# Attention and a gated MLP on one core: scores in bursts of three units, a lent pair of banks

## The chip, the core and the metric

The kernel runs on one core of a Trainium2 chip. A core has a matmul engine (TensorE, shown as PE, with its weight loads as PEld), a vector engine (VectorE, DVE), an activation engine (ScalarE, ACT), a general engine (GpSimd, POOL), and a queue that issues most transfers (SyncE, SP). Each engine takes its own instructions in the order in which they are written; between engines, semaphores say when a result is there or a buffer free. Matmuls write their results into PSUM, which here is used as eight banks of 128 partitions x 512 float32; only ACT and DVE read them from there in this kernel. The metric is the device time of one execution in microseconds (us); lower is better.

## The reference

Grouped attention (16 query heads, 4 key heads, 384 tokens, head size 64, batch 8), whose output is the input of an MLP with a spatial gate:

```python
scores = scale * np.matmul(q, k.transpose(0, 1, 3, 2))
attn = np.exp(scores - scores.max(-1, keepdims=True))
attn = attn / (attn.sum(-1, keepdims=True) + 1e-09)
x = np.matmul(attn, v)               # heads side by side: B x S x 1024
h = np.maximum(x @ w_in, 0.0)        # 1024 -> 1024
u, v = h[..., :512], h[..., 512:]
v_n = (v - mean(v)) / np.sqrt(var(v) + 1e-06)
v_s = np.einsum('ts,bsd->btd', w_spatial, v_n) + b_spatial[None, :, None]
out = (u * v_s) @ w_out              # 512 -> 1024
```

## The kernel before

Everything is float16 on the matmul engine. The order of the work is written out by hand: one loop over steps `n`, each of which issues, on PE, a piece of the attention and then a number of columns of matmuls of the MLP of an earlier batch, out of a generator (`stream`, `run_fill`).

**Attention.** A batch has six sets `m` (token tile `qt`, half of the heads `j`), and a set has three units `t`, one for each tile of 128 keys, so 18 units a batch (`NU`) and 144 in all. `scores(n)` (L224) makes one unit: two matmuls of 64 rows x 512 columns, one in each half of the array, into a tile of two banks, and one exp of 1024 columns on ACT. `weigh(b, m, hh)` (L242) is done twice for each set: twelve matmuls of 65 columns into the one bank of `ps_av`, then on DVE a reciprocal `r` and a multiplication that writes `x16`. Its weights are the exps, all three units of a set.

In the first batch one unit is issued a step; from step 18 on, two units at every even step (L599 to L601).

**The gated MLP.** For each batch: three `v_tile`s (L288; eight matmuls of 512 columns, relu on DVE, then mean and variance on DVE), four `u_block`s (L358; eight matmuls of 384 columns, relu on ACT; the first batch has three `u_tile`s instead, L337), in the middle of the first of them `normal` (L311: Ln and Exp of three columns on ACT, `nmr` on DVE, three normalisations on POOL), four `gate`s (L375; three matmuls of 384 columns, an addition on DVE, a multiplication on POOL), and six `project`s (L395; four matmuls of 512 columns, a copy on DVE for the first half of a row and on ACT for the second, and the transfer out). The first v-tile of the next batch stands between the gates and the projections (L447). "A group" is below the matmuls that fill one bank before it is read out.

**PSUM.** Eight banks: two tiles of two banks for the scores (`ps_sc`, L59), one for the weighing (L60), and three single banks, in turn, for all else (`ps_ck`, L61): the transposes of q, k, x and of the spatial weights, the warm-up matmuls and the groups of the MLP. A pool hands its buffers out in a ring, so a tile waits for the last reader of the tile that had its buffer before.

**Around it.** `keep_warm` (L502) issues four matmuls into a bank that nobody reads, at steps 0 to 9, 14 and 15. Loads, casts and transposing transfers are issued at fixed steps (`at`, L489) on POOL's and SP's queues; the PE transposes of the first batches at fixed steps too (`turn_at`, L494).

Of the kernel before, what the change touches and what calls it, by code (L numbers as in the profile page):

```python
# [12 lines left out]
ALU = mybir.AluOpType  # L13
# [4 lines left out]
def kernel(  # L18
# [37 lines left out]
    moe = ctx.enter_context(tc.tile_pool(name="moe", bufs=2))  # L56
    small = ctx.enter_context(tc.tile_pool(name="small", bufs=4))
    ops = ctx.enter_context(tc.tile_pool(name="ops", bufs=4))
    ps_sc = ctx.enter_context(tc.tile_pool(name="ps_sc", bufs=2, space=PSUM))  # L59
    ps_av = ctx.enter_context(tc.tile_pool(name="ps_av", bufs=1, space=PSUM))  # L60
    ps_ck = ctx.enter_context(tc.tile_pool(name="ps_ck", bufs=3, space=PSUM))  # L61


    stage = {}
# [118 lines left out]
        return qTs[b, j]  # L183

    def k_transposes(b, j, eng):
        ps = ps_ck.tile([P, S], FP16, name=f"kps_{b}_{j}", tag="ck")
        for t in range(NT):
            nc.tensor.transpose(
                ps[:, t * P : (t + 1) * P],
                k16s[b][:, j, t].rearrange("p h d -> p (h d)"),  # L190
                ident16,
            )
        eng(k_tile(b)[:, j], ps)

    def q_transposes(b, j, t, *engs):
        w = G // len(engs)
        for x, eng in enumerate(engs):
            ps = ps_ck.tile([P, w * P], FP16, name=f"qps_{b}_{j}_{t}_{x}", tag="ck")
            for i in range(w):
                nc.tensor.transpose(  # L200
                    ps[:, i * P : (i + 1) * P],
                    q16s[b, j][:, t, x * w + i].rearrange("p h d -> p (h d)"),
                    ident16,
                )
            eng(q_tile(b, j)[:, t, x * w * P : (x + 1) * w * P], ps)
# [13 lines left out]
        )  # L219


    aTs, avs, x16s, xts = {}, {}, {}, {}

    def scores(n):  # L224
        b, r = divmod(n, NU)
        m, t = divmod(r, NT)
        qt, j = divmod(m, 2)
        if t == 0:
            aTs[b, m] = att.tile([P, NT, 2, 512], FP16, name=f"aT_{b}_{m}", tag="aT", bufs=3)
        sc = ps_sc.tile([P, 2, 512], FP32, name=f"sc_{b}_{m}_{t}", tag="sc")  # L230
        for hh in range(2):
            half = slice(hh * D, (hh + 1) * D)
            nc.tensor.matmul(  # L233
                sc[:, hh],
                kTs[b][half, j, t * P : (t + 1) * P],
                qTs[b, j][half, qt],
                start=True,
                stop=True,
            )
        nc.scalar.activation(aTs[b, m][:, t], sc, AF.Exp, scale=scale)  # L240

    def weigh(b, m, hh):  # L242
        qt, j = divmod(m, 2)
        av = ps_av.tile([P, G, D + 1], FP32, name=f"av_{b}_{m}_{hh}", tag="av")
        for i in range(G):
            for t in range(NT):
                nc.tensor.matmul(  # L247
                    av[:, i, :],
                    aTs[b, m][:, t, hh, i * P : (i + 1) * P],
                    v1[b % 2][:, 2 * j + hh, t, 0 : D + 1],  # L250
                    start=(t == 0),
                    stop=(t == NT - 1),
                )
        if m == 0 and hh == 0:
            x16s[b] = att.tile([P, NT, NB, P], FP16, name=f"x16_{b}", tag="x16")
        r = small.tile([P, G, 1], FP32, name=f"r_{b}_{m}_{hh}", tag="r")
        nc.vector.reciprocal(r, av[:, :, D : D + 1])  # L257
        blk = 4 * j + 2 * hh
        nc.vector.tensor_tensor(  # L259
            x16s[b][:, qt, blk : blk + 2].rearrange("p k (i d) -> p (k i) d", i=2),  # L260
            av[:, :, 0:D],
            r.to_broadcast([P, G, D]),
            ALU.mult,
        )
# [5 lines left out]

    def x_transposes(b, m):
        qt, j = divmod(m, 2)
        ps = ps_ck.tile([P, 4, P], FP16, name=f"xps_{b}_{m}", tag="ck")
        for i in range(4):
            nc.tensor.transpose(ps[:, i], x16s[b][:, qt, 4 * j + i], ident16)  # L275
        nc.vector.tensor_copy(x_tile(b)[:, qt, 4 * j : 4 * j + 4], ps)
# [11 lines left out]
    def v_tile(b, st):  # L288
        if st == 0:
            mvs[b] = small.tile([P, NT, 2], FP32, name=f"mv_{b}", tag="mv")  # L290
            v_rs[b] = []
        pv = ps_ck.tile([P, 512], FP32, name=f"pv_{b}_{st}", tag="ck")
        for kt in range(NB):
            nc.tensor.matmul(  # L294
                pv,
                x_tile(b)[:, st, kt],
                w_in16[:, kt, DH:DFF],
                start=(kt == 0),
                stop=(kt == NB - 1),
            )  # L300
            if kt < NB - 1:
                yield 512
        vr = moe.tile([P, DH], FP32, name=f"vr_{b}_{st}", tag="vr", bufs=4)
        nc.vector.tensor_scalar(vr, pv, 0.0, None, op0=ALU.max)  # L304
        stats = small.tile([P, 6], FP32, name=f"stats_{b}_{st}", tag="stats")
        nc.vector.bn_stats(stats, vr)  # L306
        nc.vector.bn_aggr(mvs[b][:, st, :], stats)
        v_rs[b].append(vr)
        yield 512
# [26 lines left out]

    def u_tile(b, st):  # L337

        pu = ps_ck.tile([P, NM, P], FP32, name=f"pu_{b}_{st}", tag="ck")
        for m in range(NM):  # L340
            for kt in range(NB):
                if st == 1 and m == 1 and kt == 0:
# [7 lines left out]
                )  # L350
                if m < NM - 1 or kt < NB - 1:
                    yield P
        nc.vector.tensor_scalar(
            uT_tile(b)[:, :, st * P : (st + 1) * P], pu, 0.0, None, op0=ALU.max
        )
        yield P

    def u_block(b, m):  # L358
        pu = ps_ck.tile([P, 512], FP32, name=f"pu_{b}_{m}", tag="ck")
        for kt in range(NB):  # L360
            nc.tensor.matmul(  # L361
                pu[:, 0:S].rearrange("p (t s) -> p t s", t=NT),
                w_in16[:, kt, m * P : (m + 1) * P],
                x_tile(b)[:, :, kt],
                start=(kt == 0),
                stop=(kt == NB - 1),
            )
            if m == 0 and kt == 3:
                normal(b)
            if kt < NB - 1:  # L370
                yield S
        nc.scalar.activation(uT_tile(b)[:, m, :], pu[:, 0:S], AF.Relu)
        yield S

    def gate(b, m):  # L375
        if m == 0:
            gTs[b] = moe.tile([P, NM, S], FP16, name=f"gT_{b}", tag="gT")
        psp = ps_ck.tile([P, 512], FP32, name=f"psp_{b}_{m}", tag="ck")
        for st in range(NT):
            nc.tensor.matmul(  # L380
                psp[:, 0:S],
# [5 lines left out]
            if st < NT - 1:  # L387
                yield S
        g = moe.tile([P, S], FP32, name=f"g_{b}_{m}", tag="g", bufs=4)
        nc.vector.tensor_tensor(g, psp[:, 0:S], bias_b, ALU.add)  # L390
        by = nc.vector if b == B - 1 and m % 2 else nc.gpsimd
        by.tensor_tensor(gTs[b][:, m, :], g, uTs[b][:, m, :], ALU.mult)  # L392
        yield S
# [1 line left out]
    def project(b, tt, half):  # L395
# [5 lines left out]

        cuts = (512, 768, 1024) if last and tt == NT - 1 and half else (512 * half, 512 * half + 512)
        for i, (lo, hi) in enumerate(zip(cuts, cuts[1:])):
            po = ps_ck.tile([P, 512], FP32, name=f"po_{b}_{tt}_{half}_{i}", tag="ck")
            for m in range(NM):
                nc.tensor.matmul(  # L406
                    po[:, 0 : hi - lo],
# [4 lines left out]
                )  # L412
                if m < NM - 1:
                    yield hi - lo
            (nc.scalar.copy if half and not i else nc.vector.tensor_copy)(  # L415
                osb[:, lo:hi], po[:, 0 : hi - lo]
            )
            if last:
                nc.sync.dma_start(rows[:, tt, lo:hi], osb[:, lo:hi])
# [58 lines left out]
        w_stage["ws16"] = t16  # L478

    def ws_transposes(st):  # L480
        ps = ps_ck.tile([P, S], FP16, name=f"wps_{st}", tag="ck")
# [15 lines left out]

    by_dve, by_act = nc.vector.tensor_copy, nc.scalar.copy

    warm = ps_ck.tile([P, 512], FP32, name="warm", tag="ck")  # L500

    def keep_warm(n):  # L502
        for _ in range(n):
            nc.tensor.matmul(warm[:, 0:P], ident16, ident16, start=True, stop=True)  # L504

# [27 lines left out]
    for j in range(2):  # L533
        for t in (1, 2):
            turn_at(3 * (2 * t + j) - 3, q_transposes, 0, j, t, by_dve)
    for n in (*range(10), 14, 15):
        turn_at(n, keep_warm, 4)
    at(9, cast_k, 1, pool)
    at(10, cast_q, 1, 0, pool)
# [48 lines left out]
    def run_fill(cols):  # L588
        nonlocal owed
        owed += cols  # L590
        while owed > 0:
            owed -= next(fill, 1e9)

    for n in range(total + 6):
        for f, args in todo.pop(n, []):
            f(*args)
        if n + 1 < NU:
            scores(n + 1)
        elif n >= NU and n % 2 == 0 and n < total:  # L599
            scores(n)  # L600
            scores(n + 1)  # L601
        for hh in range(2):
            b, r = divmod(n - 3 - hh, NU)
            if n >= 3 + hh and r % 3 == 0 and b < B:
                weigh(b, r // 3, hh)
        for f, args in turns.pop(n, []):
            f(*args)
        if n < NU + 3:

            run_fill(HV / 4 if 10 <= n < 14 else 2 * HV / 5 if 16 <= n else 0)  # L610
        elif n < 2 * NU + 4:
            run_fill((4 * HV + NM * NT * S + 6 * NM * 512) / (NU + 4 - 3))
        else:
            run_fill(COLS / NU)
    for _ in fill:
        pass
    assert not todo and not turns
# [1 line left out]
_INS = ['q', 'k', 'v', 'moe_w_in', 'moe_w_spatial', 'moe_b_spatial', 'moe_w_out']  # L619
# [26 lines left out]
```

## Time and profile before

| | |
|---|---|
| runs, median (lowest to highest) | 253.76 us (253.17 to 254.05), 3 runs |
| the profiled execution | 253.12 us |
| its span, first to last instruction | 251.3 us |
| instructions in it | 6020 |
| granted TensorE clock, mean over the span | 1.00 |
| exps (L240) | 144, 139.6 us busy on ACT |
| scores (L233) | 288 matmuls, 45.0 us busy on PE |

The profile is one execution. Its span is 1.8 us shorter than its time, which has what lies around the program. A row of a group gives busy time, the mean duration of one in ns, and then the idle time of the engine just before it and who ended it. Matmuls are pipelined: one takes 379 ns from start to end at 512 columns while the next one starts much earlier, so the mean duration is not the step. The chain of waits follows the work that ended last backwards and gives time to each instruction from its start to the next one's.

### The profile page before, as it was taken

How to read it: one execution, taken by the hardware profiler on the slowest of the kernel's cores; microseconds unless marked ns; L12 is line 12 of the kernel's file. 1: busy time of each engine (PE TensorE's matmuls, PEld its weight loads, DVE VectorE, ACT ScalarE, POOL GpSimd, SP SyncE). 2: the span in 40 equal slices, each digit the busy share in tenths (PEclk: the TensorE clock that was granted, in tenths of full speed). 3: DMA queues.
4: the chain of work that ended last, by engine and by line, in shares of the span. 5: the costliest groups of instructions: out<-in, count | busy, mean ns of one | idle time of the engine just before them, and what ended most of it. 6: DMA issues, size and time to landing. Idle time of an engine off the chain costs nothing.

```text
span 251.3 us, 6020 instructions
## 1 busy us (share of the span) xinstructions
PE 240.9 (96%) x2430; PEld 125.7 (50%) x2430; DVE 139.7 (56%) x368; ACT 168.2 (67%) x215; POOL 98.3 (39%) x142
## 2 busy tenths in 40 slices
PE   7898998999999999999999999999999999999883
PEld 7564657534455444544455445544455445544442
DVE  2455776854626755474626655474636655465462
ACT  3996566678696687768696687768696687741211
POOL 2698837871035701392036602391035003320320
PEclk9999999999999999999999999999999999999999
DMA  7999998999289964997399956997392452106006
GB/s 179 268 285 251 301 285 238 297 224 265 88 182 330 171 230 85 266 233 216 121 199 324 185 200 66 281 253 227 111 171 49 111 183 44 34 12 250 0 22 232
DMA packets 73981, 46.93 MB, mean 187 GB/s; under 512 B 48113, under 2 KB 68913, under 8 KB 73953
## 3 DMA queue, kind: packets, MB, share of 16 engines
q1 hardware_dynamic: 68832, 37.63, 59.4%
q0 software_dynamic: 4080, 8.65, 13.8%
q8 instruction: 19, 0.31, 0.5%
q10 hardware_dynamic: 1040, 0.26, 0.5%
q14 instruction: 10, 0.07, 0.1%
HBM read 25.95 MB, written 12.58 MB: 153 GB/s over the span
## 4 chain that ended last, share of the span: by engine, by line
PE 87%; DVE 7%; issue 1%; ACT 1%; POOL 1%; POOLq 0%; DVEq 0%
PE av L247 17%; PE pv L294 16%; PE sc L233 15%; PE po L406 15%; PE pu L361 13%; PE psp L380 6%; PE warm L504 3%; DVE stats L306 2%; DVE vr L304 2%; DVE x L259 2%; PE pu L344 1%; PE qps L200 1%; ACT aT L240 1%; POOL vn L322 1%; PE xps L275 1%
## 5 line engine op out<-in xcount | busy, mean ns | idle before, releaser
L240 ACT ACTIVATE aT<-sc 128x1024 f16<-128x1024 f32 x144 | 139.6, 1021 | 52.9 <-PE sc L233 52.7
L247 PEld LDWEIGHTS <-aT 128*128 128x128 f16 x1152 | 43.4, 97 | 32.9 <-DVE x L259 12.9
L322 POOL TENSOR_SCALAR vn<-vr,rstd,nmr 128x512 f16<-128x512 f32 x24 | 18.1, 767 | 99.6 <-DVE r L257 85.7
L247 PE MATMUL av<-v,aT 128*128 128x65 f16 x1152 | 52.3, 194 | 1.6 <-DVE x L259 1.2
L294 PE MATMUL pv<-w_in,xt 128*128 128x512 f16 x192 | 49.5, 378 | 0.0
L257 DVE RECIPROCAL r<-av 128x4 f32<-128x4 f32 x96 | 17.1, 178 | 58.3 <-PE av L247 57.8
L406 PE MATMUL po<-w_out,gT 128*128 128x512 f16 (+1 forms) x196 | 48.2, 375 | 0.9 <-POOL gT L392 0.9
L233 PE MATMUL sc<-qT,kT 64*128 64x512 f16 x288 | 45.0, 382 | 0.7 <-ACT aT L240 0.4
L259 DVE TENSOR_TENSOR x<-av,r 128x256 f16<-128x256 f32 x96 | 40.7, 424 | 3.4
L361 PE MATMUL pu<-xt,w_in 128*128 128x384 f16 x224 | 41.7, 326 | 0.0
L392 POOL TENSOR_TENSOR gT<-g,uT 128x384 f16<-128x384 f32 x30 | 26.5, 914 | 29.4 <-DVE g L390 29.4
L361 PEld LDWEIGHTS <-w_in 128*128 128x128 f16 x224 | 20.2, 97 | 14.7 <-issue 2.5
L406 PEld LDWEIGHTS <-gT 128*128 128x128 f16 x196 | 17.0, 97 | 19.4 <-issue 2.9
L170 POOL CAST q<-q 128x768 f16<-128x768 f32 (+1 forms) x36 | 24.9, 732 | 3.1 <-DMA q<-in_q_dram 3.1
L415 DVE COPY osb<-po 128x512 f32<-128x512 f32 (+1 forms) x25 | 16.8, 671 | 11.6 <-PE po L406 11.6
L294 PEld LDWEIGHTS <-xt 128*128 128x128 f16 x192 | 16.2, 97 | 13.5 <-issue 0.7
L415 ACT COPY osb<-po 128x512 f32<-128x512 f32 (+1 forms) x24 | 13.9, 580 | 12.4 <-PE po L406 12.3
L304 DVE TENSOR_SCALAR vr<-pv 128x512 f32<-128x512 f32 x24 | 16.5, 687 | 10.2 <-PE pv L294 10.0
L233 PEld LDWEIGHTS <-kT 64*128 64x128 f16 x288 | 8.9, 94 | 26.6 <-issue 24.4
L380 PE MATMUL psp<-wsT,vn 128*128 128x384 f16 x96 | 19.6, 326 | 0.6 <-POOL vn L322 0.6
L390 DVE TENSOR_TENSOR g<-psp,bias_b 128x384 f32<-128x384 f32 x32 | 16.4, 552 | 5.9 <-PE psp L380 5.9
L306 DVE BATCH_NORM_STATS2 stats<-vr 128x6 f32<-128x512 f32 x24 | 16.7, 695 | 0.8
(49 smaller groups left out, 125.8 us busy)
## 6 DMA issues: line engine op xcount, KB each, us to landing
out_dram<-osb SPq DMA_DIRECT2D x21, 512.0 KB, 2.9
q<-in_q_dram SPq DMA_DIRECT2D x10, 768.0 KB, 7.2
q<-in_q_dram POOLq DMA_DIRECT2D x4, 768.0 KB, 10.4
v<-in_v_dram SPq DMA_DIRECT2D x6, 384.0 KB, 8.7
w_in<-in_moe_w_in_dram POOLq DMA_DIRECT2D x4, 512.0 KB, 9.7
k<-in_k_dram SPq DMA_DIRECT2D x5, 384.0 KB, 4.2
out_dram<-osb SPq DMA_DIRECT2D x5, 256.0 KB, 2.0
q<-in_q_dram SPq DMA_DIRECT2D x2, 512.0 KB, 7.2
```

The lines of the kernel that those rows point to most:

```text
L170: f(q16s[b, j][:, lo:hi, :, hh, :], src[:, hh, lo:hi])
L233: nc.tensor.matmul(sc[:, hh], kTs[b][half, j, t * P : (t + 1) * P], qTs[b, j][half, qt], start=True, stop=True,)
L240: nc.scalar.activation(aTs[b, m][:, t], sc, AF.Exp, scale=scale)
L247: nc.tensor.matmul(av[:, i, :], aTs[b, m][:, t, hh, i * P : (i + 1) * P], v1[b % 2][:, 2 * j + hh, t, 0 : D + 1], start=(t == 0), stop=(t ...
L259: nc.vector.tensor_tensor(x16s[b][:, qt, blk : blk + 2].rearrange("p k (i d) -> p (k i) d", i=2), av[:, :, 0:D], r.to_broadcast([P, G, D]) ...
L294: nc.tensor.matmul(pv, x_tile(b)[:, st, kt], w_in16[:, kt, DH:DFF], start=(kt == 0), stop=(kt == NB - 1),)
L306: nc.vector.bn_stats(stats, vr)
L361: nc.tensor.matmul(pu[:, 0:S].rearrange("p (t s) -> p t s", t=NT), w_in16[:, kt, m * P : (m + 1) * P], x_tile(b)[:, :, kt], start=(kt == 0 ...
L380: nc.tensor.matmul(psp[:, 0:S], v_ns[b][st][:, m * P : (m + 1) * P], wsT16[:, st, :], start=(st == 0), stop=(st == NT - 1),)
L392: by.tensor_tensor(gTs[b][:, m, :], g, uTs[b][:, m, :], ALU.mult)
L406: nc.tensor.matmul(po[:, 0 : hi - lo], gTs[b][:, m, tt * P : (tt + 1) * P], w_out16[:, m, lo:hi], start=(m == 0), stop=(m == NM - 1),)
L415: (nc.scalar.copy if half and not i else nc.vector.tensor_copy)(osb[:, lo:hi], po[:, 0 : hi - lo])
```

## The change

The banks are dealt out anew. The scores get three tiles of two banks, the weighing keeps one bank, and one single bank is left for the rest:

```diff
-    ps_sc = ctx.enter_context(tc.tile_pool(name="ps_sc", bufs=2, space=PSUM))
+    ps_sc = ctx.enter_context(tc.tile_pool(name="ps_sc", bufs=3, space=PSUM))
     ps_av = ctx.enter_context(tc.tile_pool(name="ps_av", bufs=1, space=PSUM))
-    ps_ck = ctx.enter_context(tc.tile_pool(name="ps_ck", bufs=3, space=PSUM))
+    ps_ck = ctx.enter_context(tc.tile_pool(name="ps_ck", bufs=1, space=PSUM))
```

From step 18 on, the three units of a set are issued together at every third step. All PE transposes take their bank from the scores' pool (`tag="sc"`), the warm-ups from the single bank, and those at steps 14 and 15 are left out:

```diff
-        elif n >= NU and n % 2 == 0 and n < total:
-            scores(n)
-            scores(n + 1)
+        elif n >= NU and n % 3 == 0 and n < total:
+            clk["pe"] += 0.19
+            for i in range(3):
+                scores(n + i)
+                if i == 0:
+                    pair["ready"] = clk["act"] + 0.2
...
-    for n in (*range(10), 14, 15):
+    for n in range(10):
         turn_at(n, keep_warm, 4)
```

A group of the MLP now asks a planner for its bank. The planner keeps a rough clock of PE, ACT and DVE while the program is written, and chooses between the two banks of a fourth tile of the scores' pool, the pair, which is taken anew after each burst, and the single bank (`None`):

```diff
+    def bank(cols, name):
+        now = clk["pe"]
+        dur = cols * COL
+        due = now + ahead_of["cols"] * COL + (0.4 if ahead_of["weigh"] else 0.0)
+        best = None
+        for i in (0, 1, None):
+            if i is None:
+                wait = max(0.0, lone["free"] - now)
+            else:
+                begin = max(now, pair["ready"], pair["free"][i])
+                end = begin + dur + (0.4 if ahead_of["weigh"] else 0.0)
+                wait = begin - now
+                if ahead_of["more"]:
+                    wait += max(0.0, end + 0.5 - due)
+                    if end > due:
+                        wait += 100.0
+            if best is None or wait < best[0] - 0.05:
+                best = (wait, i)
+        i = best[1]
+        if i is None:
+            t = ps_ck.tile([P, 512], FP32, name=name, tag="ck")
+            clk["pe"] = max(now, lone["free"])
+        else:
+            if pair["tile"] is None:
+                pair["tile"] = ps_sc.tile([P, 2, 512], FP32, name=f"pair_{name}", tag="sc")
+            t = pair["tile"][:, i]
+            clk["pe"] = max(now, pair["ready"], pair["free"][i])
+        used[name] = i
+        return t
```

The reader of a group is chosen by the same clock: whichever of ACT and DVE would end first, where both can (the gate's addition stays on DVE):

```diff
+    def read_out(name, cols, by_act, by_dve):
+
+        now = clk["pe"] + 0.2
+        ends = {}
+        if by_act:
+            ends["act"] = max(now, clk["act"]) + 0.17 + 0.00083 * cols
+        if by_dve:
+            ends["dve"] = max(now, clk["dve"]) + 0.1 + 0.00115 * cols
+        e = min(ends, key=ends.get)
+        (by_act if e == "act" else by_dve)()
+        clk[e] = ends[e]
...
-        pv = ps_ck.tile([P, 512], FP32, name=f"pv_{b}_{st}", tag="ck")
+        name = f"pv_{b}_{st}"
+        pv = bank(HV, name)
...
-        nc.vector.tensor_scalar(vr, pv, 0.0, None, op0=ALU.max)
+        read_out(
+            name,
+            512,
+            lambda: nc.scalar.activation(vr, pv, AF.Relu),
+            lambda: nc.vector.tensor_scalar(vr, pv, 0.0, None, op0=ALU.max),
+        )
```

`u_tile`, `u_block`, `gate` and `project` are changed in the same manner. The columns of the MLP that a step issues are as before (`dealt` has the same numbers). The pair is dropped after each burst and taken again by the next group that wants it:

```diff
+        if n < NU or n % 3 == 0:
+            pair["tile"] = None
...
+        ahead_of["more"] = n < total - 3
+        ahead_of["cols"] = owed + sum(dealt(i) for i in range(n, n + 3 - n % 3 if n >= NU else n + 1))
```

More of the change, by code (lines that the diff above doesn't have):

```diff
@@ L185, in k_transposes @@
     def k_transposes(b, j, eng):
-        ps = ps_ck.tile([P, S], FP16, name=f"kps_{b}_{j}", tag="ck")
+        ps = ps_sc.tile([P, S], FP16, name=f"kps_{b}_{j}", tag="sc")
         for t in range(NT):
@@ L197, in q_transposes @@
         for x, eng in enumerate(engs):
-            ps = ps_ck.tile([P, w * P], FP16, name=f"qps_{b}_{j}_{t}_{x}", tag="ck")
+            ps = ps_sc.tile([P, w * P], FP16, name=f"qps_{b}_{j}_{t}_{x}", tag="sc")
             for i in range(w):
@@ L219, in q_turn @@
         )
+    COL = 0.00042
+    clk = dict(pe=0.0, act=0.0, dve=0.0, av=0.0)
+    lone = dict(free=0.0)
+    pair = dict(tile=None, ready=0.0, free=[0.0, 0.0])
+    ahead_of = dict(cols=0.0, weigh=False, more=True)
+    used = {}
+    def bank(cols, name):
[37 more added lines that the diff above has]
+        clk[e] = ends[e]
+        i = used[name]
+        if i is None:
+            lone["free"] = ends[e] + 0.1
+        else:
+            pair["free"][i] = ends[e] + 0.1
     aTs, avs, x16s, xts = {}, {}, {}, {}
@@ L240, in scores @@
         nc.scalar.activation(aTs[b, m][:, t], sc, AF.Exp, scale=scale)
+        clk["pe"] += 0.22
+        clk["act"] = max(clk["act"], clk["pe"] + 0.25) + 1.03
     def weigh(b, m, hh):
@@ L253, in weigh @@
                 )
+        clk["pe"] = max(clk["pe"], clk["av"]) + 0.39
+        clk["dve"] = max(clk["dve"], clk["pe"] + 0.2) + 0.65
+        clk["av"] = clk["dve"] + 0.1
         if m == 0 and hh == 0:
@@ L272, in x_transposes @@
         qt, j = divmod(m, 2)
-        ps = ps_ck.tile([P, 4, P], FP16, name=f"xps_{b}_{m}", tag="ck")
+        ps = ps_sc.tile([P, 4, P], FP16, name=f"xps_{b}_{m}", tag="sc")
         for i in range(4):
@@ L303, in v_tile @@
         vr = moe.tile([P, DH], FP32, name=f"vr_{b}_{st}", tag="vr", bufs=4)
-        nc.vector.tensor_scalar(vr, pv, 0.0, None, op0=ALU.max)
+        read_out(
[4 more added lines that the diff above has]
+        )
+        clk["dve"] = max(clk["dve"], clk["pe"] + 0.8) + 0.9
         stats = small.tile([P, 6], FP32, name=f"stats_{b}_{st}", tag="stats")
@@ L337, in u_tile @@
     def u_tile(b, st):
-        pu = ps_ck.tile([P, NM, P], FP32, name=f"pu_{b}_{st}", tag="ck")
+        name = f"pu_{b}_{st}"
+        pu = bank(HV, name).rearrange("q (m s) -> q m s", m=NM)
         for m in range(NM):
@@ L352, in u_tile @@
                     yield P
-        nc.vector.tensor_scalar(
-            uT_tile(b)[:, :, st * P : (st + 1) * P], pu, 0.0, None, op0=ALU.max
+        u = uT_tile(b)[:, :, st * P : (st + 1) * P]
+        read_out(
+            name,
+            512,
+            lambda: nc.scalar.activation(u, pu, AF.Relu),
+            lambda: nc.vector.tensor_scalar(u, pu, 0.0, None, op0=ALU.max),
         )
@@ L358, in u_block @@
     def u_block(b, m):
-        pu = ps_ck.tile([P, 512], FP32, name=f"pu_{b}_{m}", tag="ck")
+        name = f"pu_{b}_{m}"
+        pu = bank(NB * S, name)[:, 0:S]
         for kt in range(NB):
             nc.tensor.matmul(
-                pu[:, 0:S].rearrange("p (t s) -> p t s", t=NT),
+                pu.rearrange("p (t s) -> p t s", t=NT),
                 w_in16[:, kt, m * P : (m + 1) * P],
@@ L371, in u_block @@
                 yield S
-        nc.scalar.activation(uT_tile(b)[:, m, :], pu[:, 0:S], AF.Relu)
+        u = uT_tile(b)[:, m, :]
+        read_out(
+            name,
+            S,
+            lambda: nc.scalar.activation(u, pu, AF.Relu),
+            lambda: nc.vector.tensor_scalar(u, pu, 0.0, None, op0=ALU.max),
+        )
         yield S
@@ L377, in gate @@
             gTs[b] = moe.tile([P, NM, S], FP16, name=f"gT_{b}", tag="gT")
-        psp = ps_ck.tile([P, 512], FP32, name=f"psp_{b}_{m}", tag="ck")
+        name = f"psp_{b}_{m}"
+        psp = bank(NT * S, name)
         for st in range(NT):
@@ L389, in gate @@
         g = moe.tile([P, S], FP32, name=f"g_{b}_{m}", tag="g", bufs=4)
-        nc.vector.tensor_tensor(g, psp[:, 0:S], bias_b, ALU.add)
+        read_out(
+            name, S, None, lambda: nc.vector.tensor_tensor(g, psp[:, 0:S], bias_b, ALU.add)
+        )
         by = nc.vector if b == B - 1 and m % 2 else nc.gpsimd
@@ L403, in project @@
         for i, (lo, hi) in enumerate(zip(cuts, cuts[1:])):
-            po = ps_ck.tile([P, 512], FP32, name=f"po_{b}_{tt}_{half}_{i}", tag="ck")
+            name = f"po_{b}_{tt}_{half}_{i}"
+            po = bank(NM * (hi - lo), name)
             for m in range(NM):
@@ L414, in project @@
                     yield hi - lo
-            (nc.scalar.copy if half and not i else nc.vector.tensor_copy)(
-                osb[:, lo:hi], po[:, 0 : hi - lo]
+            to, src = osb[:, lo:hi], po[:, 0 : hi - lo]
+            read_out(
+                name,
+                hi - lo,
+                lambda: nc.scalar.copy(to, src),
+                lambda: nc.vector.tensor_copy(to, src),
             )
@@ L480, in ws_transposes @@
     def ws_transposes(st):
-        ps = ps_ck.tile([P, S], FP16, name=f"wps_{st}", tag="ck")
+        ps = ps_sc.tile([P, S], FP16, name=f"wps_{st}", tag="sc")
         for tt in range(NT):
@@ L498 @@
     by_dve, by_act = nc.vector.tensor_copy, nc.scalar.copy
-    warm = ps_ck.tile([P, 512], FP32, name="warm", tag="ck")
     def keep_warm(n):
+        warm = ps_ck.tile([P, 512], FP32, name="warm", tag="ck")
         for _ in range(n):
@@ L591, in run_fill, with dealt @@
         while owed > 0:
-            owed -= next(fill, 1e9)
+            c = next(fill, 1e9)
+            owed -= c
+            clk["pe"] += min(c, 512) * COL
+            ahead_of["cols"] -= c
+    def dealt(n):
+        if n < NU + 3:
+            return HV / 4 if 10 <= n < 14 else 2 * HV / 5 if 16 <= n else 0
+        if n < 2 * NU + 4:
+            return (4 * HV + NM * NT * S + 6 * NM * 512) / (NU + 4 - 3)
+        return COLS / NU
     for n in range(total + 6):
@@ L596 @@
             f(*args)
+        if n < NU or n % 3 == 0:
+            pair["tile"] = None
         if n + 1 < NU:
+            clk["pe"] += 0.19
             scores(n + 1)
-        elif n >= NU and n % 2 == 0 and n < total:
-            scores(n)
-            scores(n + 1)
+            pair["ready"] = clk["pe"]
+        elif n >= NU and n % 3 == 0 and n < total:
+            clk["pe"] += 0.19
+            for i in range(3):
[4 more added lines that the diff above has]
+        ahead_of["cols"] = owed + sum(dealt(i) for i in range(n, n + 3 - n % 3 if n >= NU else n + 1))
         for hh in range(2):
@@ L605 @@
                 weigh(b, r // 3, hh)
+        ahead_of["weigh"] = n % 3 == 0 and NU <= n < total + 3
         for f, args in turns.pop(n, []):
             f(*args)
[L608 to L616, printed above, removed]
+            clk["pe"] += 0.25
+        run_fill(dealt(n))
+    ahead_of["more"] = False
+    for c in fill:
+        clk["pe"] += c * COL
     assert not todo and not turns
```

## The prediction

> **What bounds the kernel now.** First the busy rows of the page: TensorE (PE) is busy for 96% of the span at full granted clock, ACT for 67%, DVE for 56%.
>
> ```profile
> PE 240.9 (96%) x2430; PEld 125.7 (50%) x2430; DVE 139.7 (56%) x368; ACT 168.2 (67%) x215; POOL 98.3 (39%) x142
> ...
> PEclk9999999999999999999999999999999999999999
> ```
>
> Second, busy time by stage (columns: window, its length, then PE, PEld, DVE, ACT, POOL). From 60 to 222 us PE has no holes; they lie in 20 to 60 us (1.6 + 0.7 us) and in the tail, where 29.0 - 23.7 = 5.3 us are idle, 3.4 of them behind the last matmul. So about 4.2 us of waits are all that PE has now; the rest of the end is set by how many matmul steps it issues.
>
> ```profile
> 20.00:40.00 20.00, 18.45 (x260) 11.76 (x257) 14.19 (x41) 12.16 (x16) 12.10 (x17) 1.00 1.11 281
> 40.00:60.00 20.00, 19.31 (x231) 10.52 (x230) 12.60 (x34) 14.11 (x16) 14.72 (x21) 1.00 1.01 236
> ...
> 222.00:251.00 29.00, 23.72 (x147) 11.93 (x145) 15.38 (x31) 6.76 (x14) 4.09 (x5) 1.00 0.29 109
> ```
>
> Third, the chain of waits gives the step from one matmul to the next: 1.94/9 = 0.215 us at 512 columns, 0.97/6 = 0.162 at 384.
>
> ```profile
> 146.97 1.94 PE pv L294 x9
> ...
> 154.49 0.97 PE pu L361 x6
> ```
>
> Fourth, the timeline of PE around one burst of scores (start, length, instruction).
>
> ```profile
> 142.61 0.38 PE L406 MATMUL po<-w_out,gT 128*128 128x512 f16 x1
> 142.92 0.61 PE L233 MATMUL sc<-qT,kT 64*128 64x512 f16 x4
> 143.46 1.25 PE L406 MATMUL po<-w_out,gT 128*128 128x512 f16 x5
> ```
>
> The last projection starts at 142.61 and the first score at 142.92: 0.31, not 0.215. The four half-array matmuls run in pairs, so they should take 2 x 0.215 = 0.43; the next full-array one comes after 0.54. Entering and leaving the half-array form costs 0.10 + 0.11 = 0.2 us a burst.
>
> **What it removes.** Units 18 to 143 come now in 63 bursts of two and then in 42 of three: 21 x 0.2 = 4.2 us saved. Units 0 to 17 stay single. Eight warm-up matmuls at steps 14 and 15 go too; ACT sets the pace there, so 0 (at most 8 x 0.06 = 0.5).
>
> **What it moves.** Read-outs are dealt between ACT and DVE: in the changed program ACT has 11 of the 24 v-tiles but only 16 of the 28 u-blocks, and four or five more copies. Its net is about 11 x 0.59 - 12 x 0.49 + 6 x 0.59 = +4 us in a span where it idles a third: nothing by itself. SP's instructions keep their order, and no DMA changes its step.
>
> **What it adds: waits on PE.** Before, three gated banks turn round, so a group of matmuls starts two groups after the last use of its bank and the read-out is hidden behind the next group. Now there is one lone bank and a lent pair. In the built order of the changed program I looked at what the first matmul of each group waits for. Two things stand there. Where consecutive groups get the lone bank, the second waits for the read-out of the first. And the pair is one tile: the first matmul into its second bank waits for the read-out of its first bank, though it writes elsewhere. So a lent pair works as one bank. All later PE work, the next scores among it, is queued behind the waiting matmul, and behind the scores the exps on ACT.
>
> The price of such a wait: a matmul ends 0.379 - 0.215 = 0.164 after its successor could have started (the same at 384: 0.326 - 0.162), then the reader begins, runs, and PE resumes.
>
> ```profile
> L406 PE MATMUL po<-w_out,gT 128*128 128x512 f16 x188 | 47.3, 379 | 0.9 <-POOL gT L392 0.9
> ...
> L361 PE MATMUL pu<-xt,w_in 128*128 128x384 f16 x224 | 41.7, 326 | 0.0
> ```
>
> ```profile
> L259 DVE TENSOR_TENSOR x<-av,r 128x256 f16<-128x256 f32 x96 | 40.7, 424 | 3.4
> L257 DVE RECIPROCAL r<-av 128x4 f32<-128x4 f32 x96 | 17.1, 178 | 58.3 <-PE av L247 57.8
> L306 DVE BATCH_NORM_STATS2 stats<-vr 128x6 f32<-128x512 f32 x24 | 16.7, 695 | 0.8
> L304 DVE TENSOR_SCALAR vr<-pv 128x512 f32<-128x512 f32 x24 | 16.5, 687 | 10.2 <-PE pv L294 10.0
> L390 DVE TENSOR_TENSOR g<-psp,bias_b 128x384 f32<-128x384 f32 x32 | 16.4, 552 | 5.9 <-PE psp L380 5.9
> ```
>
> ```profile
> L415 ACT COPY osb<-po 128x512 f32<-128x512 f32 x23 | 13.5, 589 | 11.7 <-PE po L406 11.6
> L372 ACT ACTIVATE uT<-pu 128x384 f16<-128x384 f32 x28 | 13.1, 489 | 3.6 <-PE pu L361 3.6
> L314 ACT ACTIVATE rstd<-mv,eps_t 128x3 f32<-128x3 f32 x8 | 2.4, 297 | 6.1 <-DVE mv L307 6.1
> ```
>
> The two hand-overs are in the timeline of 150.5 to 152.9: the exp starts at 152.86, 0.43 after its scores, whose matmul takes 0.39 (0.04 to a reader); the weighing at 151.02 waits for the x that ends at 150.96 (0.06 back to PE).
>
> ```profile
> 150.54 0.42 DVE L259 TENSOR_TENSOR x<-av,r 128x256 f16<-128x256 f32 x1
> 151.02 0.18 PEld L247 LDWEIGHTS <-aT 128*128 128x128 f16 x4 [0.51 <-DVE x L259]
> 152.43 0.60 PE L233 MATMUL sc<-qT,kT 64*128 64x512 f16 x4
> 152.86 1.02 ACT L240 ACTIVATE aT<-sc 128x1024 f16<-128x1024 f32 x1 [1.59 <-PE sc L233]
> ```
>
> So 0.164 + 0.04 + reader + 0.06: 0.85 us for a 512 read by ACT, 0.95 by DVE's relu, 0.82 for a gate's add, 0.75 for a 384 relu on ACT. ACT's relu of 512 has no row; between the relu of 384 (0.489) and the copy of 512 (0.589) I take the copy, which has its size.
>
> The places, counted in that order:
> - Gate 1 behind gate 0, in one pair, batches 0 to 6. DVE first does r and x of a weighing: counted from its last matmul's start, r at 0.23, x at 0.45, the add at 0.79, its end at 1.34, PE at 1.40; PE was ready after 0.03 + 2 x 0.162. Wait 1.05, 7 times: 7.4.
> - Gate 3 behind gate 2, and the next batch's first v-tile behind gate 3, all in the lone bank: 14 x 0.82 = 11.5.
> - A projection behind a projection or a v-tile (token tile 1 in the pair for batches 1 to 5; twice the lone bank in batch 0): 7 x 0.85 = 6.0.
> - The third unit of the set that starts after the first u-block, batches 2 to 7: it takes the pair's banks, whose relu stands on ACT behind Ln and Exp of rstd, and these behind vr, stats and mv on DVE. From the last weighing matmul of that stretch: vr at 0.79, then 0.687, 0.695, 0.182 (mv), 0.297, 0.204 (the second rstd) and 0.489, some 0.15 of hand-overs: PE at 3.5. PE's own work until then is 2 x 0.215 + 9 x 0.162 + 0.10 + 2 x 0.22 = 2.4 or 2.5. Wait 1.0, 6 times: 6.0. It needs no cover before because the burst there needs no bank of a u-block.
> - Batch 1's stage: four u- and v-tiles behind each other in the lone bank, 0.95 + 3 x 0.85 = 3.5; four groups of transposes, now in the score banks, wait for an exp, between 0 and its 1.02, 0.45 taken: 1.8.
> - The tail, behind the last burst: everything goes on in one pair, each group behind the read-out of the one before: 11 x 0.85 (three projections, two v-tiles, the first u-block, five last projections), 4 x 0.75 (two u-blocks and two gates behind a relu), and once 0.3 where a gate in the lone bank lies between: 12.7.
>
> Sum of waits: 7.4 + 11.5 + 6.0 + 6.0 + 5.3 + 12.7 = 48.9. The 4.2 us of PE holes that the second view shows lie in the same stages and are taken up by these. Sum: -4.2 + 48.9 - 4.2 = +40.5. On the profiled execution's 253.1 us that is 293.6; the median lies 0.6 above it: 294.
>
> **A rule weighed.** All rows above have the clock at 1.00, also in the tail with its holes. The Trainium skill (TensorE: Matmul & The Clock Gate, "A second HAM failure mode: psum-queue depth-cycling") tells of a kernel that cycled through PSUM banks and whose short idles between groups made the clock drop and return; that is this tail's pattern. By the rows the tail costs 12.7 us; by the rule its matmuls would also run at a lower clock for part of the time.
>
> **Rivals.**
> - The pair's banks are independent after all (the wait I read on the second bank is met early). Then the 7.4, five of the projections' 0.85 and the tail's 12.7 go: 294 - 24 = 270. For it: they are separate banks. Against: the built order names the first bank's reader at each of these places.
> - Faster: the read-outs hide behind weighings and other groups, and the saved switches remain, 253.8 - 4.2 = 249.6. For it: ACT and DVE idle a third or more. It decides only if all waits together stay under 8.4 us, a sixth of those counted. Against: in 20 places a group directly follows in the same bank with nothing between, and idle readers do not shorten 0.82.
> - The clock falls where PE idles half the time. In the tail some 16 groups of 0.85 us would take up to twice that, 294 + 14 = 308; matmuls at twice their time are in the trace, in its first microseconds (the chain of waits has 27 warm-ups in 3.06 us, 0.113 each, and later 12 of the same size in 0.67, 0.056 each). For it: gaps of 0.85 each 1.7 us. Against: in the present tail gaps of up to a microsecond leave the granted clock at 1.00 and the step at 0.215.
>
> **How the numbers follow.** The waits as counted: 0.85, at 294. Its own ends: without the transposes (-1.8), without DVE's queue at gate 1 (-1.6) and with half the third unit's wait (-3), 287 or 288; with the transposes at 1.02 (+2.3), exps ahead of the projections' copies on ACT (+1.5) and weighings that wait for DVE (the 0.5 of the row above, some six times, +3), 301. Independent banks 0.06, clock 0.07, faster 0.02. Range 286 to 302. No change is told from a change at about 0.3%. Faster 0.02, same 0.01, slower 0.97.
>
> **What would show it.** Right: PE's idle rises to some 45 us, put down to ACT's osb, DVE's g and ACT's uT ahead of projections, gates, v-tiles and scores; the period of a batch (now 146.97 - 118.91 = 28.06 between the same v-tiles in the chain of waits) grows to about 32; the tail's PE row shows alternating holes; 42 bursts of six scores. Wrong: a batch period under 30, a tail without holes, or a granted clock under 1.

## The result, and the profile after

| | before | changed |
|---|---|---|
| median (lowest to highest) | 253.46 us (253.06 to 254.05), 4 runs | 295.38 us (295.1 to 295.8), 4 runs |
| span of the profiled execution | 251.3 us | 293.8 us |
| period of a batch in the steady part | 28.06 us | 32.30 us |
| steps that PE lost beyond its own pace, from 1 us on | 11.0 us | 58.9 us |

The changed kernel is slower: the ratio is 1.165, with an interval of 1.162 to 1.169. The last row (the "lost steps" below) adds, over all neighbouring matmuls, what the distance of their starts has beyond the step (0.215 us at 512 columns, 0.162 at 384) and beyond the 0.1 us of a change between the full and the half array. The two score matmuls of a unit start together and count as one step; distances that are less than 0.03 us too long are left out.

First the busy rows of the page of the changed kernel. PE does the same work (245 us against 241, as its modelled overlaps are fewer) in a longer span, so its share falls from 96 to 83%. Nobody else became the bound: the shares of DVE and ACT fell too.

```profile
span 293.8 us, 5974 instructions
## 1 busy us (share of the span) xinstructions
PE 245.0 (83%) x2422; PEld 129.2 (44%) x2422; DVE 137.8 (47%) x363; ACT 172.4 (59%) x220; POOL 98.7 (34%) x142
...
PEclk9999999999999999999999999999999999999999
```

The busy times by stage show holes of 4.0 us in 32 of the steady part, where PE had none, and of 14 us in the tail, 3.5 of them behind the last matmul, where it had 5.3. The clock stays at 1.00; it is lower only in the last 1.1 us, behind the last matmul, which makes the 0.99 of the last row.

```profile
92.00:124.00 32.00, 28.00 (x269) 13.89 (x266) 16.33 (x42) 20.18 (x26) 10.37 (x14) 1.00 0.68 170
252.00:293.80 41.80, 27.45 (x173) 12.96 (x169) 10.94 (x25) 12.75 (x23) 4.09 (x5) 0.99 0.20 76
```

The waits of the changed kernel, longest first, say who ends the holes (waiting line, the line waited for: us in total, times, longest). Nearly every one of PE's is the reader of a bank. This view gives the idle time behind the modelled end of the last matmul, so each is some 0.16 us shorter than the step that is lost.

```profile
PE pair_po L492 <- ACT osb L505: 9.9, 13, 0.9
...
PE pair_psp L463 <- DVE g L474: 6.1, 7, 0.9
...
PE pv L358 <- DVE g L474: 5.2, 7, 0.9
PE psp L463 <- DVE g L474: 5.0, 7, 0.7
...
PE sc L291 <- ACT uT L452: 4.7, 6, 0.8
```

One place in time order, from the timeline: the gates of a batch (gates 0 to 3 of the prediction). The pair's second gate starts at 150.56, right after the add of the first gate (149.96 + 0.55). The third gate, the first in the lone bank, follows at 151.04 without a wait. The fourth (152.41) and the v-tile behind it (153.78), both in the lone bank too, again start right after the add of their predecessor. That is three waits in 3.2 us.

```profile
149.96 0.55 DVE L474 TENSOR_TENSOR g<-pair_psp,bias_b 128x384 f32<-128x384 f32 x1
150.56 0.65 PE L463 MATMUL pair_psp<-wsT,vn 128*128 128x384 f16 x3 [0.87 <-DVE g L474]
...
151.04 0.65 PE L463 MATMUL psp<-wsT,vn 128*128 128x384 f16 x3
...
151.80 0.56 DVE L474 TENSOR_TENSOR g<-psp,bias_b 128x384 f32<-128x384 f32 x1
...
152.41 0.65 PE L463 MATMUL psp<-wsT,vn 128*128 128x384 f16 x3 [0.72 <-DVE g L474]
...
153.17 0.56 DVE L474 TENSOR_TENSOR g<-psp,bias_b 128x384 f32<-128x384 f32 x1 [0.81 <-PE psp L463]
153.78 0.38 PE L358 MATMUL pv<-w_in,xt 128*128 128x512 f16 x1 [0.72 <-DVE g L474]
...
154.09 0.82 PE L291 MATMUL sc<-qT,kT 64*128 64x512 f16 x6
...
154.84 0.55 PE L307 MATMUL av<-v,aT 128*128 128x65 f16 x12
```

The last two rows show that the change did what it was for. Six scores go out together: 0.31 us after the v-tile's matmul, and 0.75 us until the next full-array one, where three steps take 0.65. So a burst of three costs the same 0.10 + 0.10 us as a burst of two.

And the tail, where PE and ACT take turns within one pair, a projection every 1.7 us in place of 0.86:

```profile
284.14 1.02 PE L492 MATMUL pair_po<-w_out,gT 128*128 128x512 f16 x4 [0.68 <-ACT osb L505]
...
285.20 0.59 ACT L505 COPY osb<-pair_po 128x512 f32<-128x512 f32 x1 [1.11 <-PE pair_po L492]
285.84 1.02 PE L492 MATMUL pair_po<-w_out,gT 128*128 128x512 f16 x4 [0.67 <-ACT osb L505]
```

### The profile page after: what moved, and what is told of

It is laid out like the page before. It is cut to its first block, busy times and chain, and to the rows that moved or that the text cites. A ratio compares the mean times of both kernels' runs of the same rounds, so it can differ in the third digit from the quotient of the medians.

```text
span 293.8 us, 5974 instructions
## 1 busy us (share of the span) xinstructions
PE 245.0 (83%) x2422; PEld 129.2 (44%) x2422; DVE 137.8 (47%) x363; ACT 172.4 (59%) x220; POOL 98.7 (34%) x142
## 4 chain that ended last, share of the span: by engine, by line
PE 62%; ACT 14%; DVE 13%; issue 5%; DMA 2%; SPq 1%; POOL 1%; POOLq 0%; DVEq 0%; ACTq 0%
PE av L307 11%; PE sc L291 10%; PE pv L358 9%; PE pair_po L492 8%; ACT aT L298 7%; DVE g L474 5%; PE pu L437 5%; PE po L492 5%; PE pair_pv L358 4%; ACT osb L505 3%; PE pair_pu L437 3%; DMA q<-in_q_dram 2%; PE pu L415 2%; DVE stats L376 2%; DVE vr L372 2%
## 5 line engine op out<-in xcount | busy, mean ns | idle before, releaser
L298 ACT ACTIVATE aT<-sc 128x1024 f16<-128x1024 f32 x144 | 137.4, 1025 | 44.8 <-PE sc L291 44.7
L358 PE MATMUL pv<-w_in,xt 128*128 128x512 f16 x128 | 35.2, 378 | 5.9 <-DVE g L474 5.2
L492 PE MATMUL pair_po<-w_out,gT 128*128 128x512 f16 (+1 forms) x116 | 30.9, 374 | 10.7 <-ACT osb L505 9.9
L291 PEld LDWEIGHTS <-kT 64*128 64x128 f16 x288 | 11.9, 94 | 41.2 <-issue 34.3
L505 ACT COPY osb<-pair_po 128x512 f32<-128x512 f32 x21 | 12.4, 590 | 17.9 <-PE pair_po L492 17.9
L492 PE MATMUL po<-w_out,gT 128*128 128x512 f16 (+1 forms) x80 | 21.4, 373 | 1.4 <-ACT vr L371 0.7
L437 PE MATMUL pu<-xt,w_in 128*128 128x384 f16 x96 | 20.5, 325 | 0.0
L437 PE MATMUL pair_pu<-xt,w_in 128*128 128x384 f16 x96 | 17.6, 326 | 0.0
L463 PEld LDWEIGHTS <-vn 128*128 128x128 f16 x96 | 8.8, 97 | 19.2 <-issue 15.0
L463 PE MATMUL pair_psp<-wsT,vn 128*128 128x384 f16 x42 | 10.1, 324 | 6.1 <-DVE g L474 6.1
```

What stands on the lines that cost most here:

```text
L291: nc.tensor.matmul(sc[:, hh], kTs[b][half, j, t * P : (t + 1) * P], qTs[b, j][half, qt], start=True, stop=True,)
L358: nc.tensor.matmul(pv, x_tile(b)[:, st, kt], w_in16[:, kt, DH:DFF], start=(kt == 0), stop=(kt == NB - 1),)
L437: nc.tensor.matmul(pu.rearrange("p (t s) -> p t s", t=NT), w_in16[:, kt, m * P : (m + 1) * P], x_tile(b)[:, :, kt], start=(kt == 0), stop= ...
L463: nc.tensor.matmul(psp[:, 0:S], v_ns[b][st][:, m * P : (m + 1) * P], wsT16[:, st, :], start=(st == 0), stop=(st == NT - 1),)
L492: nc.tensor.matmul(po[:, 0 : hi - lo], gTs[b][:, m, tt * P : (tt + 1) * P], w_out16[:, m, lo:hi], start=(m == 0), stop=(m == NM - 1),)
L505: lambda: nc.scalar.copy(to, src),
```

## The experiments

The theory under test has three parts: the pair counts as one bank, because it is one tile; the third unit waits for a relu that stands behind Ln and Exp on ACT; and the saving of 0.2 us a burst is real. All ratios are against the kernel before, run beside.

**Each bank followed by itself.**

```diff
-    ps_sc = ctx.enter_context(tc.tile_pool(name="ps_sc", bufs=3, space=PSUM))
+    ps_sc = ctx.enter_context(tc.tile_pool(name="ps_sc", bufs=6, space=PSUM))
...
-                pair["tile"] = ps_sc.tile([P, 2, 512], FP32, name=f"pair_{name}", tag="sc")
-            t = pair["tile"][:, i]
+                pair["tile"] = [
+                    ps_sc.tile([P, 512], FP32, name=f"pair{x}_{name}", tag="sc") for x in range(2)
+                ]
+            t = pair["tile"][i]
...
+        for hh in range(2):
+            nc.scalar.activation(aTs[b, m][:, t, hh], sc[hh], AF.Exp, scale=scale)
```

> The changed kernel with every tile of two score banks made of two tiles of one bank (six in the ring, the exp in two halves of 512 columns), so that each bank of the lent pair is followed by itself; the planner, the bursts and the one other bank stay. Theory (the pair counts as one bank): gate 1 behind gate 0 (7 x 1.03), the projection in the pair (5 x 1.07) and the tail's 16 waits (12.7) go, the other waits stay: 295.4 - 25 = 270, within 3. Rival (four banks are too few, whoever follows them): another reader ends those waits, 288 or more.

Measured: 270.01 us (269.98 to 270.23), ratio 1.065 (1.064 to 1.067). The lost steps fall from 58.9 to 32.6 us. In the timeline the first two gates now run on without a gap (five matmuls in a row, behind a first one that stands ahead of the weighing), while the second gate in the lone bank still waits for the add of the first:

```profile
141.76 0.97 PE L468 MATMUL pair_psp<-wsT,vn 128*128 128x384 f16 x5
...
142.57 0.65 PE L468 MATMUL psp<-wsT,vn 128*128 128x384 f16 x3
...
143.45 0.55 DVE L479 TENSOR_TENSOR g<-psp,bias_b 128x384 f32<-128x384 f32 x1
144.05 0.65 PE L468 MATMUL psp<-wsT,vn 128*128 128x384 f16 x3 [0.83 <-DVE g L479]
```

The run is 25.4 us below the changed kernel. Of these, 1.5 us lie in the first batch, which takes 21.1 us from its first score to the first burst of three in place of 22.6: its transposes take one bank of the ring now and not two, and most of their waits are gone. The rest, some 24 of the 42 us, comes from the pair being one tile.

**The split of the exps alone**, a control on the kernel before (the same two edits, four one-bank tiles in the ring).

> The kernel before with the exps in two halves of 512 columns and one-bank tiles for the scores, nothing else. By the line through ACT's rows (0.489 at 384, 1.02 at 1024 columns) a half takes 0.60, about 0.07 more a unit on ACT, 10 us of ACT in all. Theory: PE sets the end, so 253.5 to 255. Rival (ACT is near its limit and the split itself costs): 258 or more, which would have to be taken off the run with banks followed one by one.

Measured: 253.93 us (253.67 to 255.2), ratio 1.0017 (1.0001 to 1.0032). In the kernel before the split gains nothing; it costs 0.4 us, hardly more than the noise. Nor does it shorten the first batch (22.3 us against 22.0).

**The tail by turns.**

```diff
+        turn[0] += 1
-        for i in (0, 1, None):
+        for i in ((0, 1, None) if ahead_of["more"] or not turn[0] % 2 else (None,)):
```

> The changed kernel, but behind the last burst the groups take the lone bank and the pair by turns. Theory: each group's read-out is hidden behind the next group, so the tail's sixteen waits (12.6 us in the trace) fall to about 1.5: 284, within 1.5; nothing ahead of the last burst moves. Rival (the readers limit the tail): unchanged, 294 to 296.

Measured: 284.42 us (284.19 to 284.57), ratio 1.122 (1.120 to 1.124); the steady period stays at 32.30. In the tail's timeline a copy now runs while the next projection fills the other bank, and the projections follow at 0.86 us:

```profile
274.04 1.03 PE L494 MATMUL po<-w_out,gT 128*128 128x512 f16 x4
...
274.90 1.03 PE L494 MATMUL pair_pv<-w_out,gT 128*128 128x512 f16 x4
275.10 0.59 ACT L507 COPY osb<-po 128x512 f32<-128x512 f32 x1 [0.28 <-PE po L494]
275.76 1.03 PE L494 MATMUL po<-w_out,gT 128*128 128x512 f16 x4
```

**Ln and Exp of rstd behind the relu** (rstd is the factor that ACT computes in `normal` from the variance). The edit takes `normal(b)` from the fourth matmul of the first u-block to the first of the second:

```diff
-            if m == 0 and kt == 3:
+            if m == 1 and kt == 0:
                 normal(b)
```

> The changed kernel with Ln and Exp of rstd issued behind the relu of the first u-block in place of ahead of it (batches 1 to 7). Theory: the third unit of that set then waits for the relu alone, which is read out 0.75 after the block while PE has 0.16 + 0.54 of other work, so its 0.94 falls to about 0.1, six times: 290, within 1. Rival (the exps on ACT, not the relu, hold the third unit): 295.

Measured: 290.43 us (290.0 to 290.59), ratio 1.146 (1.144 to 1.147). First the place in the timeline of the changed kernel: ACT has to wait for mv, then does Ln, Exp and only then the relu, and two of the burst's six matmuls come 1.39 us after the other four.

```profile
141.22 0.61 PE L291 MATMUL sc<-qT,kT 64*128 64x512 f16 x4
...
141.65 0.30 ACT L384 ACTIVATE rstd<-mv,eps_t 128x3 f32<-128x3 f32 x1 [1.82 <-DVE mv L377]
141.98 0.20 ACT L385 ACTIVATE rstd<-rstd 128x3 f32<-128x3 f32 x1
142.09 0.47 ACT L452 ACTIVATE uT<-pair_pu 128x384 f16<-128x384 f32 x1
...
142.61 0.39 PE L291 MATMUL sc<-qT,kT 64*128 64x512 f16 x2 [0.78 <-ACT uT L452]
```

With the edit the relu comes first and the six go out as one:

```profile
138.69 0.49 ACT L452 ACTIVATE uT<-pair_pu 128x384 f16<-128x384 f32 x1 [1.34 <-PE pair_pu L437]
...
138.75 0.88 PE L291 MATMUL sc<-qT,kT 64*128 64x512 f16 x6
...
139.18 0.30 ACT L384 ACTIVATE rstd<-mv,eps_t 128x3 f32<-128x3 f32 x1
```

**The same edit in the kernel before**, as a control.

> Control: the kernel before with Ln and Exp of rstd behind the relu. There no unit of scores waits for a bank of a u-block, so theory says no gain: 253 to 256 (up to a few tenths a batch worse, as nmr and the normalisations come later). Rival (the place of rstd costs in any kernel): 248 to 250.

Measured: 255.96 us (255.69 to 256.66), ratio 1.011 (1.008 to 1.013). In this kernel, where no unit of scores takes a u-block's bank, the move gains nothing: it costs 0.4 us a batch (28.43 against 28.06).

**Banks and rstd together.**

> The run with banks followed one by one (270.0) plus Ln and Exp of rstd behind the relu, nothing else. If the two causes are separate waits they add up: the third unit's six waits (4.9 us in the trace of the changed kernel) go here too, 264.8, between 264 and 266. Rival (the freed time falls into the gates' waits right behind): 268 to 270.

Measured: 265.3 us (265.28 to 265.32), ratio 1.047 (1.045 to 1.049). The two add up: 295.4 - 25.4 - 4.9 = 265.1.

**Bursts of one**, in the kernel before:

```diff
-        elif n >= NU and n % 2 == 0 and n < total:
-            scores(n)
-            scores(n + 1)
+        elif n >= NU and n < total:
+            scores(n)
```

> The kernel before with one unit in a burst from step 18 on: 126 bursts in place of 63. Theory (entering and leaving the half-array form costs 0.2 us): 63 x 0.2 = +12.6 at most, less what falls into present waits (about 4 us of PE holes): 262 to 266. Rival (the 0.2 is a hand-over that another engine hides): within 1 us of before.

Measured: 263.3 us (263.25 to 263.53), ratio 1.039 (1.037 to 1.041). The steady period grows from 28.06 to 29.70, that is 1.64 us for nine more bursts, 0.18 each. The present waits take the difference: the lost steps fall from 11.0 to 7.9 us. So the price of a burst holds, and 21 fewer are worth 3.8 us (at 0.18) to 4.2 (at 0.2).

**No lending**: all groups in the lone bank (`for i in (None,)`).

> The changed kernel without lending: all groups of the MLP in the lone bank, so nearly each waits for the read-out of the one before. About 16 groups a batch in 8 batches; in the changed kernel 53 of them have such a wait, so some 70 more at 0.82 to 0.85: theory 295 + 58 = 353, between 340 and 360. Rival (waits merge with others, as PE would wait there anyway): under 320.

Measured: 367.34 us (2 runs), ratio 1.449 (1.446 to 1.452): 7 us above the range. The busy times by stage show one reason, which the expectation did not have. The granted clock falls to 0.50 for 6.8 us after a stretch in which the gates, all in one bank, had left PE mostly idle (the column after POOL is the clock):

```profile
170.00:180.50 10.50, 8.06 (x87) 4.35 (x87) 3.28 (x10) 6.20 (x7) 1.90 (x3) 1.00 1.00 270
180.50:183.90 3.40, 1.30 (x6) 0.57 (x6) 1.75 (x4) 0.00 (x0) 1.83 (x2) 1.00 1.27 178
183.90:190.70 6.80, 6.06 (x39) 2.62 (x39) 1.16 (x3) 2.85 (x3) 5.81 (x8) 0.50 0.10 22
```

At 0.50 a step of 512 columns takes 0.43 us. The clock falls five times in this run before the last matmul, and the matmuls that start in these stretches are 13.5 us of steps at full clock, so the lower clock costs at most that much; the run lies 14 us above the 353 of the theory. The number of waits was nearly right: 75 more of over 0.4 us than in the changed kernel, where the expectation had 70.

**Bursts of two on the changed banks** (the burst, the drop of the pair and the planner's look ahead at every second step).

> The changed kernel's banks, planner and readers, but bursts of two units at every second step. Theory (the cost lies in the banks, not in the burst of three): the saving of 4.2 is gone and the pair must be back every 3.1 us in place of every 4.7, so fewer groups fit into it and more go one behind the other into the lone bank: 300 or more. Rival (the longer burst is what hurts): back to 254 to 260.

Measured: 334.97 us (2 runs), ratio 1.32. The longer burst is not what hurts; without it the same banks and planner are 40 us worse. The planner puts fewer groups into the pair (163 matmuls in place of 356), as it has to be back sooner, and 92 waits are over 0.4 us long in place of 61.

**One number of the planner.** In the run with banks and rstd:

```diff
-                    wait += max(0.0, end + 0.5 - due)
-                    if end > due:
+                    wait += max(0.0, end + 0.5 - due - 0.45)
+                    if end > due + 0.45:
```

> The run before this one with one number of the planner changed: the pair may be read until 0.45 us past the burst's start, as the third unit, not the first, takes its banks. Theory: gates 1 to 3 and the next v-tile then get banks of the pair in turn and the seven waits of gate 3 and most of the seven of the v-tile (7 x 1.0 + 7 x 0.9 = 13 in the run with banks followed one by one) shrink to some 4; batch 1's groups too, 3: 253, between 252 and 255. Rival (the third unit of the burst waits for these late read-outs in their place): 260 or more.

Measured: 253.53 us (253.29 to 254.52), ratio 1.0001 (0.9985 to 1.0017), 11.8 us below the run before it. The planner kept groups out of the pair that could have been read in time.

**Planned anew**: the run before this one, and assignments by hand, by four rules: which groups stay in the lone bank or go to the pair, and which are read by ACT.

```diff
+    force = {f"psp_{b}_1": None for b in range(1, B)} | {"pu_0_1": 0}
+    by = {"pu_0_2": "act"} | {f"pv_{b}_0": "act" for b in range(1, B)}
...
-        i = best[1]
+        i = force.get(name, best[1])
...
-        e = min(ends, key=ends.get)
+        e = by.get(name, min(ends, key=ends.get))
```

> The run with banks followed one by one, plus Ln and Exp of rstd behind the relu, plus a planner that lets the pair be read a little past the burst's start (0.45 us), gate 1 always in the lone bank, and two readers set by hand. Theory: nearly all 0.8 us waits of the gates and v-tiles are hidden, what is left of them is 1 to 2 us more than before, and the 21 saved switches show: 253.5 - 4.2 + 1 = 250, between 249 and 252, faster than before. Rival (some wait always takes the place of the one removed): 253 or more.

Measured: 251.02 us (250.75 to 251.21), ratio 0.990 (0.989 to 0.992) to the kernel before: faster than both, by 1%. Its lost steps are 13.3 us, 2.3 more than those of the kernel before (11.0). Its steady part by stage has no hole, and ACT, with the exps in halves, is at 80%:

```profile
88.00:116.00 28.00, 28.00 (x277) 14.23 (x278) 15.40 (x41) 22.48 (x46) 10.60 (x14) 1.00 0.87 201
```

Its period is 27.66 us in the steady part, 0.4 below that of the kernel before, where three fewer bursts a batch would give 0.6. Part of the saving is lost within the bursts: in two of the six bursts of a batch the sixth score matmul starts some 0.15 us behind the fifth, where the two normally start 0.004 apart. In the burst at 106.41 it starts at 107.00, right behind a gate's add that ends at 106.96. Busy times do not show such a wait.

## Why the prediction was right

The forecast was 294 us, the measured median 295.4; in its own terms +40.5 us on the profiled execution's time, against +42.5 in the spans. Each place of its count is in the trace of the changed kernel (distance of starts beyond the step):

| place | predicted | measured |
|---|---|---|
| saved bursts | -4.2 | 0.2 a burst by the burst of six above, 0.18 by the bursts of one: -3.8 to -4.2 |
| gate 1 behind gate 0 | 7 x 1.05 = 7.4 | 7 x 1.03 = 7.2 |
| gate 3, and the v-tile behind it | 14 x 0.82 = 11.5 | 12 x 0.88, 0.81, 1.03 = 12.4 |
| projections | 7 x 0.85 = 6.0 | 5 x 1.07, 0.85, 0.84 = 7.0 |
| third unit behind the relu | 6 x 1.0 = 6.0 | 6 x 0.94 = 5.6 |
| batch 1: groups; transposes | 3.5; 1.8 | 3.6; 1.9 |
| tail | 12.7 | 12.8 |

So the mechanism was right, place by place, and the number is not luck. The terms that were sized too low are small. The projections' copy stands on ACT behind an exp of the burst (0.2 us each, which the prediction had only in its upper end). A gate's add starts 0.11 us behind the end of its matmuls (152.41 + 0.65 = 153.06 to 153.17 in the timeline above) where the prediction took 0.04 from an exp; in the kernel before, too, it was 0.11 each time DVE stood waiting for a gate. And one wait was not listed: the third unit of the set behind the first v-tile in the pair, 0.15 us six times. With it the places add up to 51.4 us, where the prediction had 48.9.

The 4.2 us of present PE holes were not taken up in full: outside these places the changed kernel still loses 58.9 - 51.4 = 7.5 us of the 11.0 of the kernel before, among them 0.8 in the last projections, which wait for the gate's product (1.2 before). Lost steps and saved bursts together give 58.9 - 11.0 - 4.2 = 43.7 us, 1.2 more than the spans differ; 0.4 of this can be the eight warm-ups that are gone, the rest was not followed up.

The rivals. That the pair's banks are independent was priced at 270; the run that makes them so measured 270.0, and the changed kernel is not it. That the clock falls did not happen in this kernel (1.00 in every stage up to the last matmul), but it did in two of the experiments, no lending and the bursts of two, so the rival was a fair one. That read-outs hide and the bursts' saving remains is what the new deal of the banks can come to: the run planned anew is at 251.0, where that rival had 249.6. The rival asked for all waits together under 8.4 us, and there they are 2.3 us more than before. The changed kernel missed this because two banks were followed as one tile, because rstd stood ahead of the relu, and because the planner kept groups from the pair that it could have held.

What stays open: the run with the later due time and the run planned anew differ in all four rules at once, which were not tried one by one. That the split of the exps gains nothing was shown in the kernel before, not on the new banks.

## What to carry to other kernels

A bank that is filled again right after its own group costs the end of the last matmul, two hand-overs and the whole read-out, here 0.74 to 1.07 us on the bounding engine, however idle the readers are: count such places in the built order before adding up what the new layout saves. Where two banks are lent as one tile, look at what the first write into the second bank waits for; tracked as one, they are worth one bank. And where a burst takes a buffer that another engine must first read out, look at what stands ahead of that reader in its queue, here a Ln and an Exp of three columns that waited for a chain on DVE.

## What the runs showed of the hardware

The clock. In the run without lending, the granted clock fell to 0.50 five times between 98 and 321 us, for 6.8 us four times and 3.4 once, each time after a stretch in which the gates went one by one through one bank. In the 3.4 us before 183.9, seven-tenths of the matmul steps were missing: six matmuls of 384 columns at 0.162 are 0.97 us of 3.4, or 0.29. Counted in the same way, the 3.4 us before the other four falls had 0.29 to 0.37. In the run with bursts of two the clock fell twice, behind 0.37 and 0.39. In the changed kernel the thinnest such stretch (279.0 to 282.4, counted in steps of 3.41 us back from where its clock falls behind the last matmul) has 0.40, and the clock did not fall.

The two values agree with the Trainium skill (TensorE: Matmul & The Clock Gate, "What's actually happening"), which has a full and a half rate, set over windows of some 3.4 us. That a window with many short gaps and no long pause is enough, as the same page tells of a kernel that cycles through banks ("A second HAM failure mode: psum-queue depth-cycling"), is shown by the run without lending: its longest gap in these five stretches is 0.87 us. The border lies near 0.4 by this count and is not a sharp one: a stretch of 0.38 in the run with bursts of two (94.9 to 98.4) kept the clock.
